# Another order for the whole kernel, and the second block's selected row gathered by a register index

## The chip, the cores and the metric

The kernel runs on one core of one Trainium2 chip. The metric is the device time of one execution in microseconds (us), as the median of the runs. Before the change three runs took 164.52, 165.06 and 165.21 us; the median is 165.06.

## The reference, cut to what matters

`x` has 2048 tokens (S) of 512 numbers (D), in bf16. Two kinds of block alternate, A, B, A, B, each on a layer norm of `x` with the result added to `x`. The weights are the same in both rounds.

```python
def _A_ref(x, wqkv, wo):                # linear attention, H = 32 heads of Dh = 16
    q, k, v = ...                       # x @ wqkv, split into heads
    phi = lambda t: jnp.where(t > 0, t + 1, jnp.exp(t)) + 1e-6
    pq, pk = phi(q), phi(k)
    kv = jnp.einsum("bhsd,bhse->bhde", pk, v)
    z = jnp.einsum("bhsd->bhd", pk)
    num = jnp.einsum("bhqd,bhde->bhqe", pq, kv)
    den = jnp.einsum("bhqd,bhd->bhq", pq, z)[..., None] + 1e-6
    return (num / den) ... @ wo

def _B_ref(x, w_r, w_gate, w_up, w_down):   # one token of 2048 goes through an FFN
    r = x @ w_r
    idx = jnp.argsort(-r, axis=-1)[:, :1]
    x_sel = ...                         # row idx of x
    y = (silu(x_sel @ w_gate) * (x_sel @ w_up)) @ w_down      # F = 1792
    y = y * sigmoid(r[idx])
    return x + (y added to row idx)

x = x + _A_ref(_layernorm(x), ...);  x = x + _B_ref(_layernorm(x), ...)
x = x + _A_ref(_layernorm(x), ...);  x = x + _B_ref(_layernorm(x), ...)
```

## The kernel before, in words

**Layout.** The 2048 tokens are 16 tiles of 128 (`x_tok[:, t, :]`, tokens on partitions). `xn_tok` holds the normalised tiles, `xnT[0]` and `xnT[1]` the transposed ones for block 0 and block 1, `pqT` the transposed phi(q), `pk` a ring of six phi(k) tiles. In PSUM six banks (0 to 5) go round for everything short, and two (6 and 7) are held by accumulations.

**How the order is made.** Each piece of work is an operation of the recorder `Sched` (`add`), with the tiles that it reads and writes. `replay` puts all 1047 operations in the order of a list of numbers, `ORDER`, and gives each PSUM buffer the bank that the string `BANKS` names. `assign_sync` then makes one stream per engine and the semaphore waits between streams, and `emit_engine` writes the streams out. So each engine, and the DMA queue of SyncE (SP), runs its operations strictly in the order of `ORDER`; whoever waits holds up everything behind it on that engine. The names below are those that the code gives operations, with the tile or group number: `A0k13` is block 0's key product of tile 13.

**Start and block 0, keys (`ln0`, `T_pe`, `T_dma`, `kv_tile`).** SP loads `x` in four pieces, the three 512x512 parts of `wqkv` (wk, wv, wq), `wo` and the router weight. For each tile VectorE (DVE) takes the statistics (L825, L827), ScalarE (ACT) the scale; the normalised tile comes from DVE for tiles 0 to 3 (L814) and from GpSimd (POOL, L818) for the other twelve, for pairs of tiles at a time. Tiles 0 to 3 are transposed by TensorE (PE, L804), the other twelve by a DMA transpose on SP (L435, `A0T4` to `A0T15`), which can be issued once POOL has made the tile. The key product (L618, four 128x512 matmuls) needs the transposed tile; then phi: ACT's exp (L552, `E`), POOL's min (L554, `min`), DVE's max and add (L556, `phi`). In block 0 no value product is made: `gmm` (L641, L645) adds the Gram product of the normalised tile with phi(k) into four banks, with a column of ones for z. These banks are complete after all 16 tiles.

**Block 0, queries to output.** Query products in groups of four tiles (L781, `A0q{group}_{chunk}`, phi as above); the denominator of a group (`den`, L906), whose reciprocal goes through DRAM to all partitions (`rd_scr`, `rb_sb`) and is multiplied into `pqT` (L925, `qd`). `kv_out` makes the kv product from the Gram banks (`GT`, then L715 with wv), masks it (`kvTe`, L719), and `m_out` folds `wo` in (L758, `Mw`). Output tiles (`out_tile`, L950; the router's columns ride along, L544), the residual (L975, `res`) and the sum of squares (L981). `ln_mid` makes the layer norm before the second half, with POOL's tiles and DMA transposes again (`A1T`).

**FFN weights.** w_gate, w_up and w_down come in six pieces of 0.92 MB (`ldwg0`, `ldwg1`, `ldwu0`, ...), on SP too. They may be issued once `A0T15` has landed (the argument `after=[hold]`).

**Block B of the first round** (`b_front(0, ...)`, `coupling`) runs beside block 1's key and value products: the largest router value over 16 tiles (DVE MAX8 and FIND_INDEX8), over partitions by a PE transpose of the maxima, the same again; a one-hot column; POOL loads the tile index into a register and copies the selected tile to `xg` (L1133), and PE gathers the row from it (L1141, `B0gather`); `tots` (L1174), `xm`, `xsel`; the gate and up rows on PE (L1222, `B0row_g`, `B0row_u`); the down row; then the change of one token is patched into block 1 as a rank-2 update of the kv sums (`Crank2`) and added to `x` by POOL (`Cxpatch`).

**The tail: block B of the second round** (`cand_front`, `b_front(1, ...)`, `final_row`). When the last two output tiles are done, the router row is complete and the FFN of the selected token is all that is left. The row of the token is gathered in two parts. `cand_front` searches the first `NA = 12` tiles alone, ahead of time: MAX8 (L1071), the transpose of the maxima (L1073), FIND_INDEX8 (L1075, L1079), a one-hot table (`oha`, L1080), and 48 one-column matmuls over all 12 tiles (L1090). `b_front(1, ...)` searches all 16 (L1099 to L1108) and gathers from the last four tiles by 16 one-column matmuls (L1146). A fourth statistic, a flag of the first 12 tiles, tells whether the candidate is the token; `gx` joins the parts. Then `xsel`, 112 one-column matmuls for gate and up (L1204), 112 for the down row (L1283), the row's copy (L1435) and its store at a row index that SP loads into a register (L1440, L1445). That store waits for all eight output stores.

Of the kernel before, what the change touches and what calls it, by code (L numbers as in the profile page):

```python
# [6 lines left out]
dt = mybir.dt  # L7
# [4 lines left out]
P = 128  # L12
# [13 lines left out]
3 24 0 11 19 25 54 18 1 30 20 7 21 12 56 31 33 27 2 61 9 55 10 8 53 76 6 57 78 58 77 79 62 80 81 63 82 64 85  # L26
65 83 66 60 84 99 67 86 101 68 59 100 102 69 154 103 104 87 105 70 88 106 164 71 72 155 73 107 23 90 165 74
156 169 75 89 91 108 157 92 4 159 93 110 170 166 109 94 158 167 160 97 134 29 168 171 98 132 161 172 184 95
123 173 96 133 135 162 136 137 189 185 112 111 186 138 145 163 190 141 187 179 113 22 121 142 139 114 115 188
124 116 180 143 191 140 146 117 192 174 144 181 39 147 193 175 118 122 119 182 148 125 227 149 176 40 126 196  # L30
120 152 177 183 228 41 127 153 222 229 47 262 223 230 150 5 178 48 263 151 202 264 306 224 265 231 203 128 225
207 204 129 246 205 208 226 209 130 210 232 197 247 131 206 38 49 233 310 237 234 32 311 248 211 235 307 238
308 28 249 239 217 309 240 236 218 195 50 258 242 219 15 259 220 241 260 243 26 261 244 212 245 254 213 200
221 214 194 255 215 256 250 13 257 266 251 199 216 252 34 51 267 253 268 270 315 312 269 331 271 316 274 332
272 52 286 275 273 333 198 390 287 334 290 276 201 391 35 282 392 277 288 291 393 294 14 289 313 292 283 278
46 314 295 284 293 298 279 296 285 335 317 280 299 297 281 300 302 318 394 435 303 301 325 323 436 326 304 319
437 321 305 320 438 327 322 483 324 42 338 484 328 329 336 346 485 339 330 337 486 340 396 347 349 43 397 348
341 343 439 350 342 402 398 351 344 370 408 395 345 403 487 399 372 409 373 374 405 371 375 400 404 441 352
376 442 401 447 354 377 440 410 443 444 406 378 355 379 356 380 411 489 357 453 383 445 358 407 488 450 384
359 381 454 360 361 446 353 413 492 362 479 44 365 451 414 382 455 448 495 363 452 366 490 415 569 491 416 417  # L40
493 501 364 523 418 480 412 419 496 420 570 498 421 502 449 422 494 562 368 426 499 423 456 497 458 555 571 45
427 572 548 556 386 544 528 563 559 557 389 549 428 558 459 552 460 457 550 429 461 560 573 564 551 462 500
424 545 594 553 431 385 463 481 425 387 504 464 465 554 574 466 580 565 469 527 503 506 367 566 467 475 36 507
470 369 508 37 509 505 477 473 524 581 576 510 529 468 430 471 530 587 577 511 525 519 521 567 16 472 578 601
434 588 579 531 512 561 513 590 532 514 602 520 660 517 533 597 534 546 661 535 518 667 664 536 595 583 537
668 662 665 540 591 670 568 598 618 592 541 584 515 593 671 615 619 672 585 474 611 538 586 673 575 516 620
675 622 616 543 674 599 676 612 582 432 680 677 539 604 542 600 613 678 621 589 605 681 653 683 682 623 686
679 606 687 625 691 688 614 684 608 607 626 689 627 596 609 690 632 743 696 717 646 633 722 654 685 603 634
694 692 610 628 647 643 476 697 695 635 648 699 655 703 720 700 719 701 639 704 693 644 705 702 617 649 707
706 708 657 698 709 640 710 711 656 624 641 658 712 666 716 642 650 713 714 744 526 659 651 715 636 723 724  # L50
725 522 726 637 629 727 728 732 729 17 652 730 638 731 547 645 741 735 748 736 630 737 752 738 749 739 776 750
753 751 760 754 777 478 756 778 779 631 757 740 755 772 761 758 813 814 762 768 759 773 718 812 763 764 769
774 829 770 765 775 788 830 771 766 784 831 721 767 789 832 815 867 785 669 790 780 868 786 791 792 869 787
781 870 816 482 793 742 782 804 745 794 783 817 796 746 795 805 833 824 797 905 825 820 906 798 821 800 806
907 799 822 801 818 908 807 808 819 871 826 802 823 827 733 663 828 809 835 834 841 810 803 837 838 811 836
943 842 909 847 944 388 839 945 844 849 873 946 875 843 879 872 845 848 885 874 846 880 840 851 855 911 876
850 881 852 912 734 853 910 882 854 886 947 859 913 877 920 887 858 883 878 914 860 921 884 861 917 888 747
922 915 864 890 923 916 893 863 918 891 949 866 892 919 433 856 955 889 948 924 931 951 897 950 925 952 898
896 927 894 902 926 956 895 900 928 958 929 971 957 932 857 972 953 862 930 962 933 966 899 959 954 865 991
901 934 960 967 935 992 993 968 963 969 904 970 982 964 995 903 980 983 994 973 997 981 965 975 984 996 986  # L60
1001 998 961 1002 1003 936 999 976 1005 939 1004 1007 1006 987 1008 937 1011 1016 940 1017 974 938 1015 942
977 1018 1012 1000 985 941 1022 1009 988 1023 1024 1014 1033 1025 1013 989 1019 1040 990 1041 1020 1026 978
1021 979 1027 1028 1029 1035 1030 1042 1036 1031 1034 1037 1032 1038 1043 1039 1044 1045 1010 1046
"""
BANKS = "2403150522641073114052325233233533225255235115320324135406723415020315045210301352254130541121053023253414550523104221121142345331250413420510350421143216203317204426531407436254125010354"
# [186 lines left out]
def bass_interleave_layers__linear_attn_block__moe_arch_mod__prompt_kernel(  # L252
# [13 lines left out]
    with ExitStack() as es:  # L266
# [9 lines left out]
        NA = 12  # L276
# [102 lines left out]
        m8a = SB("m8a", [P, 8], BF)  # L379
        i8a = SB("i8a", [P, 8], dt.uint32)  # L380
        g8a = SB("g8a", [P, 8], F32)
        gi8a = SB("gi8a", [P, 8], dt.uint32)
        tifa = SB("tifa", [P, 1], F32)
        ohta = SB("ohta", [P, NA], F32)
        oha = SB("oha", [P, NA], BF)
        gca = SB("gca", [P, NC_D], F32)
        gx = SB("gx", [P, NC_D], F32)
# [32 lines left out]
        reg_sp = es.enter_context(nc.sync.register("reg_sp"))  # L420

# [71 lines left out]
        C("pool", lambda e: e.memset(stat[1][:, 3, :], 0.0), ["flag"], est=100)  # L493
        C("pool", lambda e: e.memset(stat[1][:, 3, 0:NA], 1.0), ["flag"], est=100)
# [571 lines left out]

        def cand_front():

            sl = slice(0, NA)
            res = [f"r{g[0]}" for g in FG if g[0] < NA]  # L1070
            small(lambda e: e.max(m8a[:], r_bf[:, sl]), res, ["m8a"], "B1Amax", est=170)  # L1071
            rowb = bank()
# [8 lines left out]
                                                   scalar=iota_p[:, 0:1], in1=ohta[:], op0=ALU.is_equal,  # L1081
                                                   op1=ALU.mult), ["gi8a", "ohta", "iota_p"], ["oha"], "B1Aoh",
                  est=230)
            ga = bank()

            def gather_a(e):
                ins = None
# [483 lines left out]
```

## Time and profile before

| what | us |
|---|---|
| median of three runs | 165.06 |
| the profiled execution | 164.52 |
| its span, first to last instruction | 162.7 |
| PE busy | 148.8 |
| DVE busy | 132.9 |
| ACT busy | 106.2 |
| POOL busy | 75.2 |
| first key product of block 0 | 9.15 |
| first output tile of block 0 | 58.8 |
| first output tile of block 1 | 131.4 |
| last dense product | 149.2 |
| gate products of the tail | 154.80 |

The profile is of one execution. Its page gives the busy time of each engine, the span in 40 slices of 4.07 us (a digit is the busy share in tenths; below them the clock that TensorE was granted and the DMA engines' share), the chain of work that ended last, and groups of equal instructions with what ended the idle time before them. Other views are asked of the trace for a window of time: the timeline (start, length, engine, line, operation, output <- inputs, count), the list of waits (who waited for whom: total, times, longest), the DMA issues with their time to landing, and a table by stage. A line such as `L618` is a line of the kernel before. A helper's line stands for many operations: L571 is every small three-operand instruction of DVE. PE is the stream of matmuls, PEld that of weight loads beside it; a 512-column matmul shows as 0.38 us long, but the next one starts 0.22 us after it.

### The profile page before, as it was taken

How to read it: one execution, taken by the hardware profiler on the slowest of the kernel's cores; microseconds unless marked ns; L12 is line 12 of the kernel's file. 1: busy time of each engine (PE TensorE's matmuls, PEld its weight loads, DVE VectorE, ACT ScalarE, POOL GpSimd, SP SyncE). 2: the span in 40 equal slices, each digit the busy share in tenths (PEclk: the TensorE clock that was granted, in tenths of full speed). 3: DMA queues.
4: the chain of work that ended last, by engine and by line, in shares of the span. 5: the costliest groups of instructions: out<-in, count | busy, mean ns of one | idle time of the engine just before them, and what ended most of it. 6: DMA issues, size and time to landing. Idle time of an engine off the chain costs nothing.

```text
span 162.7 us, 3493 instructions
## 1 busy us (share of the span) xinstructions
PE 148.8 (91%) x1281; PEld 71.4 (44%) x1163; DVE 132.9 (82%) x452; ACT 106.2 (65%) x282; POOL 75.2 (46%) x125
## 2 busy tenths in 40 slices
PE   7989999999999969999999989799999979997593
PEld 2434444444434434334344535465444323332582
DVE  2999998677999999998784696784586999999951
ACT  3493453344489667977989537445779929997950
POOL 2058788744357500255875936630496710154000
PEclk9999999999999999999999999999999999999855
DMA  4999543769986767333334430000004687421360
GB/s 142 328 378 249 119 101 61 244 146 376 366 303 212 245 231 224 129 71 79 78 69 74 91 62 0 4 4 2 0 0 147 236 266 240 137 78 64 146 242 7
DMA packets 31633, 24.21 MB, mean 149 GB/s; under 512 B 15872, under 2 KB 30080, under 8 KB 31488
## 3 DMA queue, kind: packets, MB, share of 16 engines
q1 hardware_dynamic: 31616, 23.99, 49.2%
q8 instruction: 9, 0.15, 0.4%
q14 instruction: 8, 0.07, 0.2%
HBM read 14.03 MB, written 6.29 MB: 125 GB/s over the span
## 4 chain that ended last, share of the span: by engine, by line
DVE 36%; PE 32%; DMA 14%; ACT 9%; POOL 3%; issue 3%; SPq 1%; DVEq 0%
PE ps L618 11%; PE ps L781 6%; DVE x_tok L975 6%; DVE pqT L556 5%; DVE pqT L925 5%; DMA rb_sb<-rd_scr 5%; DMA x_tok<-in_A_x_dram 3%; PE ps L660 3%; PE ps L641 3%; DMA xnT<-xn_tok 3%; DMA rd_scr<-rden 3%; DVE pk L556 3%; DVE junk L851 3%; ACT Eb L552 2%; PE ps L1204 2%
## 5 line engine op out<-in xcount | busy, mean ns | idle before, releaser
L554 POOL TENSOR_SCALAR Eb<-Eb 128x512 bf16<-128x512 bf16 x64 | 40.3, 638 | 29.3 <-ACT Eb L552 28.6
L552 ACT ACTIVATE Eb<-ps 128x512 bf16<-128x512 f32 x64 | 37.1, 596 | 24.2 <-PE ps L618 15.0
L618 PE MATMUL ps<-wqkv,xnT 128*128 128x512 bf16 x153 | 38.3, 379 | 2.2 <-DVE pk L556 0.6
L950 PE MATMUL ps<-Mw,pqT 128*128 128x512 bf16 x124 | 31.1, 378 | 2.3 <-DVE pqT L925 1.4
L781 PE MATMUL ps<-xnT,wqkv 128*128 128x512 bf16 x123 | 29.6, 380 | 0.4 <-ACT Eb L552 0.2
L556 DVE SCALAR_TENSOR_TENSOR pk<-ps,Eb 128x512 bf16<-128x512 f32 x32 | 21.7, 681 | 6.7 <-POOL Eb L554 6.6
L556 DVE SCALAR_TENSOR_TENSOR pqT<-ps,Eb 128x512 bf16<-128x512 f32 x32 | 21.1, 683 | 5.6 <-POOL Eb L554 5.6
L950 PEld LDWEIGHTS ps<-Mw,pqT 128*128 128x128 bf16 x128 | 12.2, 96 | 20.9 <-DVE pqT L925 3.2
L818 POOL TENSOR_SCALAR xn_tok<-x_tok,stat,nms 128x512 bf16<-128x512 bf16 x16 | 12.4, 784 | 17.9 <-DVE nms L1017 14.7
L618 PEld LDWEIGHTS ps<-wqkv,xnT 128*128 128x128 bf16 x160 | 13.5, 97 | 15.5 <-DVE pk L556 1.3
L781 PEld LDWEIGHTS ps<-xnT,wqkv 128*128 128x128 bf16 x128 | 11.5, 97 | 13.9 <-issue 1.1
L981 ACT ACTIVATE junk<-x_tok 128x512 bf16<-128x512 bf16 x26 | 16.1, 620 | 2.2 <-DVE x_tok L975 1.8
L641 PE MATMUL ps<-pk,xn_tok 128*128 128x512 bf16 x64 | 16.4, 379 | 0.1
L544 PE MATMUL ps<-mr_hl,pqT 128*128 128x2 bf16 x96 | 15.8, 164 | 0.2
L925 DVE TENSOR_TENSOR pqT<-pqT,rb_sb 128x512 bf16<-128x512 bf16 x32 | 13.7, 447 | 0.7 <-DMA rb_sb<-rd_scr 0.7
L818 POOL TENSOR_SCALAR xn_tok<-x_tok,rs,nms 128x512 bf16<-128x512 bf16 x12 | 10.2, 850 | 8.5 <-DVE mv L827 8.0
L825 DVE BATCH_NORM_STATS2 st<-x_tok 128x6 f32<-128x512 bf16 x16 | 10.6, 677 | 2.2 <-DMA x_tok<-in_A_x_dram 2.1
L680 ACT ACTIVATE va<-ps 128x512 bf16<-128x512 f32 x16 | 9.5, 592 | 4.2 <-PE ps L618 2.7
L975 DVE SCALAR_TENSOR_TENSOR x_tok<-x_tok,ps 128x512 bf16<-128x512 bf16 x16 | 10.7, 677 | 0.0
L791 ACT ACTIVATE lnv<-mv,eps_col 128x2 f32<-128x2 f32 (+2 forms) x20 | 5.8, 291 | 7.2 <-DVE mv L827 6.4
L1426 POOL TENSOR_SCALAR xn_tok<-x_tok,us,stat 128x512 bf16<-128x512 bf16 x6 | 4.8, 803 | 11.9 <-DVE stat L571 9.9
L641 PEld LDWEIGHTS ps<-pk,xn_tok 128*128 128x128 bf16 x64 | 6.2, 97 | 7.3
(256 smaller groups left out, 232.8 us busy)
## 6 DMA issues: line engine op xcount, KB each, us to landing
rd_scr<-rden SPq DMA_DIRECT2D x8, 512.0 KB, 3.7
rb_sb<-rd_scr SPq DMA_DIRECT2D x8, 512.0 KB, 3.9
out_dram<-xn_tok SPq DMA_DIRECT2D x8, 256.0 KB, 2.1
wg<-in_B_w_gate_dram SPq DMA_DIRECT2D x2, 896.0 KB, 13.9
wu<-in_B_w_up_dram SPq DMA_DIRECT2D x2, 896.0 KB, 7.8
wd<-in_B_w_down_dram SPq DMA_DIRECT2D x2, 896.0 KB, 9.8
wqkv<-in_A_wqkv_dram SPq DMA_DIRECT2D x3, 512.0 KB, 6.0
x_tok<-in_A_x_dram SPq DMA_DIRECT2D x1, 1024.0 KB, 8.9
```

The lines of the kernel that those rows point to most:

```text
L544: ins = e.matmul(out_ap, lhsT, rhs, start=start, stop=stop, skip_group_check=True).ins
L552: A("act", lambda e: e.activation(Eb[:, i, :], src(), ACTF.Exp), reads=[b, "table"], writes=[f"E{i}"], est=600, name=name + "E")
L554: A("pool", lambda e: e.tensor_scalar(Eb[:, i, :], Eb[:, i, :], 1.0, 0.0, op0=ALU.min, op1=ALU.max), reads=[f"E{i}"], writes=[f"E{i}"], es ...
L556: return A("dve", lambda e: e.scalar_tensor_tensor(out=dst, in0=src(), scalar=1e-6, in1=Eb[:, i, :], op0=ALU.max, op1=ALU.add), reads=[b, ...
L618: ins = e.matmul(B(b), xT[:, c, t * P:(t + 1) * P], wqkv[:, c, lo:lo + D], start=(c == 0), stop=(c == NC_D - 1))
L641: e.matmul(B(kba[c]), xn_tok[:, t, c * P:(c + 1) * P], pk[:, i, :], start=first, stop=False, skip_group_check=True)
L781: ins = e.matmul(B(qb), wqkv[:, c, qc * P:(qc + 1) * P], xnT[L][:, c, tg * 512:(tg + 1) * 512], start=(c == 0), stop=(c == NC_D - 1))
L818: A("pool", lambda e: e.tensor_scalar(xn_tok[:, t, :], x_tok[:, t, :], scale[:, t:t + 1], nbias[:, t:t + 1], op0=ALU.mult, op1=ALU.add), r ...
L925: A("dve", (lambda e, tc=tc, rc=rc: e.tensor_tensor(pqT[:, :, tc], pqT[:, :, tc], rb_sb[:, i, :, rc], ALU.mult)), reads=[f"rb{i}"] + [f"pq ...
L950: ins = e.matmul(B(ob), w, Mw[:, m, :], start=(m == 0), stop=(m == NC_D - 1 and not xb))
L975: A("dve", lambda e: e.scalar_tensor_tensor(out=x_tok[:, t, :], in0=x_tok[:, t, :], scalar=scal, in1=B(ob), op0=ALU.mult, op1=ALU.add, acc ...
L981: A("act", lambda e: e.activation(junk[:, j, :], x_tok[:, t, :], ACTF.Square, accum_out=s2[L][:, t:t + 1]), reads=[f"x{t}", "table"], writ ...
```

## The change

1. **The second round's gather.** `cand_front` goes away, with its tiles, its flag (two POOL fills) and the join `gx`. `b_front(1, ...)` loads the tile index into a register of PE and gathers the row with four one-column matmuls whose weights are the selected tile, addressed by that register. The number of statistics falls from four to three.
2. **A new `ORDER` and a new `BANKS`** for all that is left, 1034 operations. Nothing else in the code differs; the lines after the removed ones move up by 11 (L618 becomes L607, and so on).

The core of the diff (the two long strings left out):

```diff
-        NA = 12
...
+        reg_pe = es.enter_context(nc.tensor.register("reg_pe"))
...
-        C("pool", lambda e: e.memset(stat[1][:, 3, :], 0.0), ["flag"], est=100)
-        C("pool", lambda e: e.memset(stat[1][:, 3, 0:NA], 1.0), ["flag"], est=100)
...
-        def cand_front():
-            ...
-            small(lambda e: e.max(m8a[:], r_bf[:, sl]), res, ["m8a"], "B1Amax", est=170)
...
-                for c in range(NC_D):
-                    for t in range(NA, NT):
-                        ins = e.matmul(B(gb)[:, c:c + 1], x_tok[:, t, c * P:(c + 1) * P], oh_bf[:, t:t + 1],
-                                       start=(t == NA), stop=(t == NT - 1))
+            def gather_reg(e):
+                e.reg_load(reg_pe, idxu[0:1, 1:2])
+                gregs["t"] = index(e, reg_pe, NT)
...
                 for c in range(NC_D):
+                    src = xg[:, c * P:(c + 1) * P] if L == 0 else x_tok[
+                        :, bass.ds(gregs["t"], 1), c * P:(c + 1) * P].rearrange("p a d -> p (a d)")
+                    ins = e.matmul(B(gb)[:, c:c + 1], src, ohp_bf[:, 0:1], start=True, stop=True)
...
+                A("pe", gather, reads=["idxu1", "ohp_bf"] + [f"x{t}" for t in range(NT)], writes=[gb], est=1050,
+                  pre=gather_reg, pre_after=[idx1_op], name=tag + "gather")
-            nr = 4
+            nr = 4 if L == 0 else 3
...
-                stt(gx[:], gca[:], tots[:, 3:4], ALU.mult, lambda: B(gb)[:, 0:NC_D], ALU.add, ["gca", "tots", gb],
-                    ["gx"], tag + "gx")
-                stt(xsel[:], gx[:], tots[:, 0:1], ALU.mult, tots[:, 1:2].to_broadcast([P, NC_D]),
-                    ALU.add, ["gx", "tots"], ["xsel"], tag + "xsel")
+                stt(xsel[:], lambda: B(gb)[:, 0:NC_D], tots[:, 0:1], ALU.mult, tots[:, 1:2].to_broadcast([P, NC_D]),
+                    ALU.add, [gb, "tots"], ["xsel"], tag + "xsel")
```

What the two orders make of the streams, by the names of the operations (`ld` are loads, `T` the DMA transposes of block 0):

```
SP before: ldx2 ldx0 ldx4 ldwk ldx8 ldwo ldwq ldwrb T6 ldwv T7 T5 T4 T13 T12 T8 T9 T15 ldwr T14
           ldwg0 T10 T11 ldwu1 ldwd1 ldwu0 ldwd0 ldwg1
SP after:  ldx0 ldx2 ldx4 ldwk ldx8 ldwq T7 T6 ldwrb T8 T5 T4 T9 T11 T15 T10 ldwo T14 T12
           ldwd1 ldwu1 ldwg0 T13 ldwd0 ldwg1 ldwu0 ldwr ldwv

PE before: pT2 pT0 pT3 k0 k2 pT1 k3 k1 kv0 kv2 k6 kv3 k7 kv1 k5 kv6 k4 kv7 k13 kv5 k12 q1_1 kv4 k8
           kv13 k9 q0_1 kv12 k14 kv8 k15 kv9 k11 kv14 q1_0 q0_0 kv15 k10 q0_3 kv11 q0_2 q1_2 kv10
           q1_3 den0 q2_0 q2_3 den1 q3_0 q2_2 q3_1 q2_1 q3_2 kvT q3_3 den2 M3 M2 M0 M1 den3
PE after:  pT0 pT2 k0 pT3 pT1 k2 k1 k3 kv0 kv2 k7 kv1 kv3 k6 k8 kv7 k5 kv6 k4 k9 kv8 kv5 k11 q0_0
           k15 kv9 kv4 k10 kv15 k14 k12 q0_1 kv11 k13 kv14 kv12 q0_2 q0_3 kv10 kv13 q1_3 q1_2 q1_0
           q1_1 den0 q2_3 q2_1 den1 q2_0 q3_0 q2_2 q3_1 q3_3 q3_2 kvT den2 M1 M2 M0 M3 den3

POOL after, during block 0's key products: ... k4min k9min xn14 xn12 k11min q0_0min k15min xn13 ...

PE, first selection, before: kv8 v13 row_g row_u k13 tr_g kv9 tr_u v15 kv10 row_y
PE, first selection, after:  gather kv8 tot v14 kv6 row_g row_u v11 tr_g k14 tr_u k12 row_y
DVE, there, before: tots Cinv u3 xm k11phi (statistic) x2c xsel k12phi
DVE, there, after:  tots xm xsel rl_g k13phi rl_u k11phi u3 x2c

PE, into block 1's outputs, before: rank2 q1_2 q1_1 q1_0 den0 ... M0 q3_3 Ctw wo1 wo0 den3 wo3
PE, into block 1's outputs, after:  rank2 kv12 q1_0 q1_1 den0 ... M0 Ctw den3 wo2 wo1 wo3
PE, tail, after:  rowmax tsel tot (register load) gather g0 u0 g7 u7 row_x row_y
DVE, tail, after: ... max mi tif gmax oht gmi (statistic) oh oht_p psf prod ohp idx1 (tile) ... tots ...
                  xsel (tile) (tile) ...
```

In these streams `pT` is a PE transpose, `k`, `v`, `q` key, value and query products, `kv` in block 0 the Gram product of a tile, `wo` an output tile.

## The prediction

> **What bounds the kernel now.** I read the page first: busy shares, the 40 slices, the chain that ended last. No engine is the bound throughout; TensorE (PE) and VectorE (DVE) take turns, and PE is rarely idle for long before the tail.
>
> ```profile
> PE 148.8 (91%) x1281; PEld 71.4 (44%) x1163; DVE 132.9 (82%) x452; ACT 106.2 (65%) x282; POOL 75.2 (46%) x125
> PE   7989999999999969999999989799999979997593
> DVE  2999998677999999998784696784586999999951
> ```
>
> PE is at 9 in nearly every slice up to the tail; DVE is loose in slices 6 to 9 (24 to 41 us) and full after. So an idle PE before 41 us is paid in full if DVE has nothing to give back, and the body's order matters more than a few small instructions.
>
> Next I read the DMA queue, because the change reorders it. First the view of DMA issues in the window 18 to 29 us, then in 29 to 32 us (name, count, us to landing), then SP's timeline.
>
> ```profile
> xnT<-xn_tok SPq DMA_TRANSPOSE x6, 2.5
> ```
> ```profile
> xnT<-xn_tok SPq DMA_TRANSPOSE x1, 4.1
> ```
> ```profile
> 26.91 1.21 SPq L435 DMA_TRANSPOSE xnT<-xn_tok  x1
> 28.17 0.58 SPq L437 DMA_DIRECT2D wg<-in_B_w_gate_dram  x1
> 29.55 4.07 SPq L435 DMA_TRANSPOSE xnT<-xn_tok  x2
> ```
>
> A block-0 transpose lands 2.5 us after its issue when nothing is ahead of it. The one issued at 29.55, behind one 0.92 MB gate load, took 4.1 and landed at 33.65. The table by stage (window, length, PE PEld DVE ACT POOL busy, clock, DMA share, GB/s) shows why: the load ramps up over two us, fills the engines, and only then does the transpose move.
>
> ```profile
> 29.00:30.00 1.00, 0.92 (x9) 0.53 (x9) 0.51 (x1) 0.12 (x1) 1.00 (x2) 1.00 0.55 56
> 31.00:32.00 1.00, 1.00 (x10) 0.51 (x9) 0.32 (x1) 0.00 (x0) 0.97 (x2) 1.00 1.05 405
> 32.00:33.00 1.00, 1.00 (x10) 0.47 (x8) 1.00 (x4) 0.59 (x1) 0.40 (x1) 1.00 1.07 309
> 38.00:39.00 1.00, 1.00 (x7) 0.41 (x5) 1.00 (x4) 0.47 (x1) 0.00 (x0) 1.00 1.08 382
> ```
>
> **Part 1, the new place of one transpose: +2.5 us.** In the changed order SP issues twelve block-0 transposes as before, but the last, of token tile 13, stands behind *three* weight loads (half of w_down, of w_up, of w_gate). Key product k13 is PE's 16th key product and needs it; PE runs in order.
>
> When does it land? One load ahead: issue of the load at 28.17 to landing of the transpose at 33.65 is 5.5 us. Each further 0.92 MB at the 373 GB/s of 36 to 44 us (same table) adds 2.5. Three ahead: 5.5 + 2 x 2.5 = 10.5 us after the first load's issue. That issue follows the transpose of tile 12, whose normalised tile POOL makes after the min of k9. In the new PE order nine key products and six Gram products precede k9; counting from 9.15 (the first key product) with PE's rows below and two input transposes of 0.33, k9 starts at 9.15 + 9 x 0.86 + 6 x 0.96 + 0.66 = 23.3 and ends at 24.2. Then exp 0.6, min 0.61, two POOL tiles at 0.78 each: 27.0; the transpose keeps SP 1.2: 28.2. With 0.4 for hops and contention the first load issues at about 28.6 and tile 13 lands at 39.1 (38.2 if the ramp hides behind the wo load, 40 if SP or POOL slip).
>
> When does PE want it? PE's timeline, the pattern of the first 40 us:
>
> ```profile
> 31.02 1.03 PE L641 MATMUL ps<-pk,xn_tok 128*128 128x512 bf16 x4
> 31.88 0.24 PE L645 MATMUL ps<-ones_bf,pk 128*128 128x1 bf16 x4
> 31.98 1.02 PE L618 MATMUL ps<-wqkv,xnT 128*128 128x512 bf16 x4
> 40.16 1.02 PE L618 MATMUL ps<-wqkv,xnT 128*128 128x512 bf16 x4
> ```
>
> A Gram product with its ones column costs 0.96 from start to start, a key or query product 0.86. The last key product of before starts at 40.16, after 15 keys, 14 Grams, 4 queries; k13 of the changed order comes after 15, 12, 2. So PE is ready at 40.16 - 2 x 0.96 - 2 x 0.86 = 36.5. It waits 39.1 - 36.5 = 2.6; I take 2.5, bounds 1.7 and 3.7. What PE saves at the front (two waits for transposes at 15 and 17 us, 0.5 together, since the wo and wv loads leave their way) is swallowed by this wait. It is not given back: from 40.16 to 54.4 PE of before shows no wait over 0.4 us, and the block's kv product, mixed matrix and output tiles all need k13's Gram. DVE does its constants during the wait, but PE is the bound there.
>
> A second price could be PE's clock. The table by stage for PE alone (window, length, busy, clock, DMA, GB/s) shows one fall, in the tail, some 4.5 us after the last dense product:
>
> ```profile
> 152.00:153.00 1.00, 1.00 (x44) 1.00 0.38 135
> 153.00:154.00 1.00, 0.79 (x22) 0.83 0.00 0
> 154.00:155.00 1.00, 0.38 (x14) 0.50 0.55 207
> ```
>
> A wait of 2.5 is shorter than that, so I add nothing. The Trainium skill (TensorE: Matmul & The Clock Gate, Part 1) says that one idle window of about 3.4 us halves PE's clock. By it a wait of 2.5 would cost nothing more, and one of 3.7 could add up to 1.7, as an estimate.
>
> The same skill (DMA: Bandwidth & Descriptors, Anatomy of one DMA) fits a transfer as 2.0 us plus bytes / 436e3. As an estimate three loads would take 2.0 + 3 x 2.1 = 8.3, tile 13 would land near 38 and the wait be 1.4; the rows of this trace say more, and they decide.
>
> **Part 2, other moves in the body: -0.8 us.** Two waits of before that the new order touches, from the lists of waits in 100 to 104 and 118 to 132 us:
>
> ```profile
> PE ps L1222 <- DVE xsel L571: 0.7, 1, 0.7
> ```
> ```profile
> PE ps L950 <- DVE pqT L925: 0.9, 1, 0.9
> ```
>
> The first: before the gate rows DVE does key product k11's phi, x2c and a statistic between xm and xsel. In the new order xsel follows xm, and PE has a value product and a kv product (0.86 + 0.23) beside them: -0.7. The second: block 1's first denominator waited 0.4 for phi; now one product fewer stands between the rank-2 patch and it, so its DRAM round trip starts earlier: -0.4 to -1.3. Against: the y row has one kv product less beside its gate (+0.3), kvT of block 0 has no query product after it (+0.1), and any new order brings waits of its own. Sum of the named ones about -1.1; taken -0.8, bounds -2.2 and +1.0.
>
> **Part 3, the selection of block 1: +0.15 us.** Removed: nine DVE operations of the candidate search and of the join, 48 + 16 one-column gathers, two POOL fills. The 48 (1.35 us) lie inside DVE's chain, where PE is idle: 0. Of the DVE ones, MAX8 and FIND_INDEX8 (0.07 + 0.15 of the chain) stand ahead of tile 15's statistics and one at 0.14 ahead of the global MAX8; the rest run while ACT makes the row scale or PE the row: -0.3 (0 to -0.5).
>
> Added: the gather now needs the tile index in a PE register. From the end of the last FIND_INDEX8 (152.59) to the gate products (154.80) takes 2.21 now. New path: oh 0.2, oht_p 0.22, PE 0.25, idx1 0.15 with two hops of 0.05 (0.9 in all, as psf, prod and ohp stand ahead of idx1 but end first), register load, four register operations with weight loads, matmul and hop 0.25, xsel 0.25. A register load on PE is not in the trace. The nearest rows, of idxu:
>
> ```profile
> L1131 POOLq TENSOR_LOAD <-idxu x1: 487/487/487, 96.8 to 96.8; - x1
> L1304 POOLq TENSOR_LOAD <-idxu x1: 303/303/303, 98.4 to 98.4; - x1
> L1440 SPq TENSOR_LOAD <-idxu x1: 575/575/575, 156.5 to 156.5; - x1
> ```
>
> I take 0.49, the load that a compute engine does first; 0.3 and 0.58 are the ends. A matmul addressed by register is not there either: a register operation takes 0.04 to 0.06 on POOL, so 4 x (0.05 + 0.1) = 0.6, at most 1.0. Sum 0.9 + 0.49 + 0.6 + 0.25 + 0.25 = 2.5, against 2.21: +0.3 (0 to +0.8). Behind the waiting load on PE stand only the FFN products, which need xsel anyway; prod's total is ahead of it. With -0.3 and a little for the smalls that follow the phis in the new order: +0.15, bounds -0.5 and +0.8. The FFN itself (112 one-column products and 112 rows back to back, 154.80 to 160.0) is the same work. The row's store waits for the output stores too: the last landed at 160.4, the row was ready at 160.34. DVE's last tiles move up, so the stores don't become the end.
>
> **Sum.** 2.5 - 0.8 + 0.15 = +1.9. The profiled execution took 164.52 (span 162.7, 1.8 around it), giving 166.4; it is the fastest of the three, 0.54 under the median. On the median of 165.06: **167.0 us**.
>
> **Rivals.**
> - *Tile 13 comes in time.* For: the three loads have no consumer before the gate rows at 102.8 us, and if a transpose passes what is queued ahead, part 1 is 0. It decides if the first load issues before 36.5 - 10.5 = 26.0, or packets of the two mix. Against: the 4.1 us row, and POOL's place of tile 12. Then the sum is -0.65: 164.4; with all of part 2's gain 163.0. Chance 0.2, half of it faster than now.
> - *The wait is longer and the clock falls.* At 3.7 the wait comes near the 4.5 us after which the tail's clock fell; each 512-column product (0.22) would take twice as long for some 3 us: +1.5 over the long end: 165.06 + 3.7 + 1.5 - 0.65 = 169.6, 168.8 with half of it. Chance 0.1. Against: PE is never idle for 2 us in the body, so no row shows it.
> - *The wait is there and is given back.* Part 1 at its low end, part 2 at its high end: 165.06 + 1.7 - 2.2 + 0.15 = 164.7, to 165.8. Chance 0.1.
> - The forecast: 0.6, own range 165.9 to 168.6.
>
> **Chances.** About 0.5% (0.8 us) is what a measurement of this kernel can tell from no change. Faster 0.10, same 0.20, slower 0.70. The range 164.2 to 168.9 leaves out the fast half of the first rival and the long end of the second.
>
> **What would show it.** Part 1: the transposes' longest time to landing is 8 us or so, and PE stands idle 2 to 3 us before one key product at 36 to 39 us, ended by a DMA of xnT. Right in kind but wrong in size if the idle is under 1.5. Wrong if no PE idle over 1 us lies before 45 us. Part 2: no wait of the gate rows for xsel. Part 3: from the last FIND_INDEX8 to the gate products 2.3 to 3.0 us.

## The result, and the profile after

The changed kernel takes 171.44 us (median of four runs, 170.37 to 171.77), the kernel before 165.07 beside it: 1.038 times as long, 95% interval 1.033 to 1.043. The prediction said 167.0, at most 168.9: right in sign, a third of the size. The profiled execution took 171.77 us, its span is 170.0 against 162.7. Ratios here and below leave out executions over 1.5% above the fastest of their kernel; medians count all of them.

From the page of the changed kernel, the lines that answer to those of before:

```profile
PE 147.9 (87%) x1220; PEld 70.4 (41%) x1102; DVE 126.1 (74%) x441; ACT 105.3 (62%) x282; POOL 75.4 (44%) x123
PE   7999499990699995989999999999999979998293
DVE  2999689577047699979983399475685998899951
PEclk9999999999599999999999999999999999999755
```

All engines but POOL have slightly less work. PE has two holes, a 4 in the fifth slice (17 to 21 us) and a 0 in the tenth (38 to 42.5 us). In the eleventh the granted clock falls (the 5), which in the kernel before it did only in the tail; its line was

```profile
PEclk9999999999999999999999999999999999999855
```

The second hole first. SP's timeline (start, length, operation, output <- input), then the DMA issues of that window (name, count, us to landing), then PE's timeline:

```profile
32.03 0.58 SPq L428 DMA_DIRECT2D wd<-in_B_w_down_dram  x1
32.65 0.56 SPq L428 DMA_DIRECT2D wu<-in_B_w_up_dram  x1
33.26 0.51 SPq L428 DMA_DIRECT2D wg<-in_B_w_gate_dram  x1
33.81 2.93 SPq L426 DMA_TRANSPOSE xnT<-xn_tok  x1
```
```profile
xnT<-xn_tok SPq DMA_TRANSPOSE x1, 9.8
```
```profile
43.77 1.86 PE L607 MATMUL ps<-wqkv,xnT 128*128 128x512 bf16 x4 [5.53 <-DMA xnT<-xn_tok]
```

The last line is key product k13, as predicted: behind three loads the transpose of tile 13 takes 9.8 us, and PE stands. But it stands 5.53 us, not 2.5. PE by stage (window, length, busy, clock, DMA, GB/s) shows what comes after:

```profile
42.00:43.00 1.00, 0.00 (x0) 1.00 0.63 75
44.00:45.00 1.00, 1.00 (x3) 0.50 1.09 348
46.00:47.00 1.00, 1.00 (x6) 0.64 1.06 383
```

The clock is halved from 43.31 to 46.72 by the record of the granted clock. The products there take nearly twice their time: k13, above, 1.86 us for 1.03.

The first hole is before k8, which needs tile 8. The list of waits, 14 to 30 us (total, times, longest):

```profile
PE ps L607 <- DMA xnT<-xn_tok: 2.2, 1, 2.2
```

The prediction had no wait there. Tile 8's transpose is issued at 15.58 and lands at 20.39: 4.8 us, though no weight load is near; only `ldwrb`, the broadcast of the router row, stands ahead of it. What held it is in the DMA issues of 17.5 to 19.5 us: the engines' busy tenths in 40 parts of the window, then a queue named "instruction" (packets, MB, share).

```profile
DMA  4649949999000009990000000001011000000000
q8 instruction: 1, 0.02, 3.0%
```

One 16 KB packet of program code, at 17.87 us for 0.96, shares the DMA engines with the transposes. In the first line the engines are busy to 18.0 us and once more for a moment at 18.25, then there is next to nothing until the end of the window. The packets of the trace, one by one, say more: none starts between 18.35 and 18.82, and from the end of the code packet (17.87 + 0.96 = 18.83) the rest start one after the other, some 0.03 us apart, up to 19.6. So the tile is held until the code packet is done. Which of the 16 engines carried what the trace does not give; that the code packet held up one of them is argued. In the kernel before such a packet comes at 18.43 and falls in a gap between two transposes (same view, 17.5 to 20 us):

```profile
DMA  9941000000000090000000000000000000000004
q8 instruction: 1, 0.02, 2.9%
```

**Where the 7.3 us of the span went**, from the starts of the same products in both traces: first output tile of block 0 at 67.69 for 58.79, 8.9 later; from there to the last output tile of block 1 87.2 for 88.8, 1.6 shorter; from there to the end 15.11 for 15.13, the same. All of the loss is made before 47 us.

### The profile page after: what moved, and what is told of

Read it like the earlier page. It is cut to its first block, busy times and chain, and to the rows that moved or that the text cites. A ratio compares the mean times of both kernels' runs of the same rounds, so it can differ in the third digit from the quotient of the medians.

```text
span 170.0 us, 3350 instructions
## 1 busy us (share of the span) xinstructions
PE 147.9 (87%) x1220; PEld 70.4 (41%) x1102; DVE 126.1 (74%) x441; ACT 105.3 (62%) x282; POOL 75.4 (44%) x123
## 4 chain that ended last, share of the span: by engine, by line
PE 40%; DVE 25%; DMA 16%; ACT 14%; issue 2%; POOL 1%; SPq 0%; DVEq 0%
PE ps L607 13%; PE ps L770 8%; DMA xnT<-xn_tok 7%; PE ps L630 6%; DMA rb_sb<-rd_scr 6%; DVE x_tok L964 6%; DVE pqT L914 5%; ACT Eb L541 4%; PE ps L526 4%; ACT junk L970 3%; DMA rd_scr<-rden 2%; DVE pqT L545 2%; ACT va L669 2%; PE ps L1161 2%; DVE pk L545 2%
## 5 line engine op out<-in xcount | busy, mean ns | idle before, releaser
L543 POOL TENSOR_SCALAR Eb<-Eb 128x512 bf16<-128x512 bf16 x64 | 39.6, 626 | 46.1 <-ACT Eb L541 45.9
L541 ACT ACTIVATE Eb<-ps 128x512 bf16<-128x512 f32 x64 | 37.6, 596 | 33.8 <-PE ps L607 23.2
L607 PE MATMUL ps<-wqkv,xnT 128*128 128x512 bf16 x155 | 39.4, 385 | 8.8 <-DMA xnT<-xn_tok 7.7
L545 DVE SCALAR_TENSOR_TENSOR pk<-ps,Eb 128x512 bf16<-128x512 f32 x32 | 21.4, 681 | 10.7 <-POOL Eb L543 10.5
L545 DVE SCALAR_TENSOR_TENSOR pqT<-ps,Eb 128x512 bf16<-128x512 f32 x32 | 21.6, 687 | 9.6 <-POOL Eb L543 9.3
L607 PEld LDWEIGHTS ps<-wqkv,xnT 128*128 128x128 bf16 x160 | 13.6, 98 | 23.8 <-issue 6.3
L807 POOL TENSOR_SCALAR xn_tok<-x_tok,stat,nms 128x512 bf16<-128x512 bf16 x16 | 13.0, 814 | 17.8 <-DVE mv L984 12.3
L914 DVE TENSOR_TENSOR pqT<-pqT,rb_sb 128x512 bf16<-128x512 bf16 x32 | 13.2, 440 | 1.6 <-DMA rb_sb<-rd_scr 1.6
L1383 POOL TENSOR_SCALAR xn_tok<-x_tok,us,stat 128x512 bf16<-128x512 bf16 x6 | 5.6, 938 | 11.4 <-DVE tot L560 9.2
L964 DVE SCALAR_TENSOR_TENSOR x_tok<-x_tok,ps 128x512 bf16<-128x512 bf16 x16 | 10.5, 677 | 0.0
## 6 DMA issues: line engine op xcount, KB each, us to landing
wg<-in_B_w_gate_dram SPq DMA_DIRECT2D x2, 896.0 KB, 11.3
```

What stands on the lines that cost most here:

```text
L541: A("act", lambda e: e.activation(Eb[:, i, :], src(), ACTF.Exp), reads=[b, "table"], writes=[f"E{i}"], est=600, name=name + "E")
L543: A("pool", lambda e: e.tensor_scalar(Eb[:, i, :], Eb[:, i, :], 1.0, 0.0, op0=ALU.min, op1=ALU.max), reads=[f"E{i}"], writes=[f"E{i}"], es ...
L545: return A("dve", lambda e: e.scalar_tensor_tensor(out=dst, in0=src(), scalar=1e-6, in1=Eb[:, i, :], op0=ALU.max, op1=ALU.add), reads=[b, ...
L607: ins = e.matmul(B(b), xT[:, c, t * P:(t + 1) * P], wqkv[:, c, lo:lo + D], start=(c == 0), stop=(c == NC_D - 1))
L807: A("pool", lambda e: e.tensor_scalar(xn_tok[:, t, :], x_tok[:, t, :], scale[:, t:t + 1], nbias[:, t:t + 1], op0=ALU.mult, op1=ALU.add), r ...
L914: A("dve", (lambda e, tc=tc, rc=rc: e.tensor_tensor(pqT[:, :, tc], pqT[:, :, tc], rb_sb[:, i, :, rc], ALU.mult)), reads=[f"rb{i}"] + [f"pq ...
```

## The experiments

Edits of the order are shown as the stream of SP or PE by name. Each kernel is measured beside runs of the kernel before on the same chip (medians 163.48, 164.83, 164.19 and 164.46 for the four groups, in the order below).

### First group: the waits one by one

```diff
 t13_first
-SP: T12 ldwd1 ldwu1 ldwg0 T13 ldwd0
+SP: T12 T13 ldwd1 ldwu1 ldwg0 ldwd0
```

> The changed kernel with one edit: the transpose of tile 13 is issued ahead of the three weight loads, not behind them. Theory (its landing at 43.6 us is a wait of 5.5 us of PE, and the halved clock after it costs 1.7 more): both go, about 171.4 - 7.2 = 164.2 us; the transpose lands some 2.5 us after its issue, PE has no idle over 1 us before that key product, the granted clock stays at 1.0. Rival (PE would have waited there or later for something else, because the new order of block 0 is slow by itself): 168 to 171 us.

Measured: 166.99, ratio 1.0144 (1.0045 to 1.0242). The wait for tile 13 is gone, but 1.4% is left. Its list of waits, and the clock in slices of 4.1 us:

```profile
PE ps L607 <- DMA xnT<-xn_tok: 2.1, 1, 2.1
PEclk9999969999999999999999999999999999999755
```

The wait that is left is the one before k8, and in this execution it cost a fall of the clock (21.55 to 24.97) which the same wait did not cost in the changed kernel. Two things more follow later: the loads end 2.4 us later, and output tiles of block 0 wait 1.4 for denominators.

```diff
 t13_warm (k13 stays behind the loads)
+        gram = next(o for o in sch.ops if o.name == "A0kv11").banks[0]
+        def warm13(e):
+            for _ in range(22):
+                e.matmul(B(gram), zeros[:, 0:P], zeros[:, :], start=False, stop=False, skip_group_check=True)
+        k13.pre = warm13
```

> The changed kernel with 22 matmuls of zeros (512 columns each, 4.8 us, added into the Gram banks, so they change no value) on PE while it waits for tile 13; the wait itself stays. Theory (the idle PE loses its clock, and that costs 1.7 us apart from the wait): no fall of the clock at 43 us, about 169.8 us. Rival (the slow clock costs nothing, since DVE and ACT set the pace after the wait): 171.2 to 171.6 us. Rival (matmuls beside the loads slow the transpose): over 172.

Measured: 168.93, 1.0312 (1.0222 to 1.0403). The clock stays at full speed up to the tail in the trace, and from k13 to the first output tile the kernel needs 1.4 us less (22.5 for 23.9). The halved clock is a cost of its own, in the trace somewhat under the 1.7 expected; the times say 1.1 us (1.0381 to 1.0312), with intervals that overlap.

```diff
 wrb_late; "both" is this and t13_first
-SP: T6 ldwrb T8 T5 T4 T9 T11
+SP: T6 T8 T5 T4 T9 ldwrb T11
-DVE: k7phi wsum ... k6phi r0d10 ... k5phi r0d14
+DVE: k7phi ... k6phi ... k5phi wsum r0d10 r0d14
```

> The changed kernel with the broadcast load of the router weight issued behind the transpose of tile 9, not ahead of that of tile 8, and DVE's first two readers of it moved behind phi of tile 5. Theory (this load holds the transpose of tile 8 up by 2.3 us, PE stands before k8, and all that follows up to the three loads comes later by as much): tile 8 lands 2.5 us after its issue, PE's wait before k8 goes from 2.2 to under 0.3, the first weight load is issued 2.3 us earlier, the wait for tile 13 stays 5.5: about 169.1 us. Rival (the wait for tile 13 absorbs it, since the loads' time is bound by transfers): 171.4.

> Both edits: tile 13 ahead of the three loads, router weight behind tile 9. Theory: 171.4 - 7.2 - 2.3 = 161.9 us, 3 us below the kernel before; what is left of the new order is then a gain of 0.9 in front, 1.6 in the body and nothing in the tail. Rival (the two waits overlap, and each repair alone already brings all that is to be had): 164.2.

Measured: 173.10, 1.0562 (1.0484 to 1.0639), and 166.62, 1.0156 (1.0071 to 1.0241). Both theories of mine fell here. With `ldwrb` out of its way k8 still came at 19.87 instead of 20.44, so the broadcast load is not the main cause of that wait. The late sums on DVE made a new wait: query product q0_0 stood 1.0 for `wmean`. In the first of the two the loads then went out at 33.05 and the clock was halved for two windows (42.55 to 49.38).

### Second group: the packet of code, the denominators, the tail

```diff
 t13_fetch: t13_first, and in warm(n)
-                for _ in range(n):
-                    ins = e.matmul(B(b), zeros[:, 0:P], zeros[:, :], start=True, stop=True)
+                for c in range(4 * n):
+                    lo = (c % 4) * P
+                    ins = e.matmul(ps[:, b.idx, lo:lo + P], zeros[:, 0:P], zeros[:, lo:lo + P], start=True, stop=True)
 t13_den: t13_first, and
-SP: T13 ldwd1 ldwu1 ldwg0 ldwd0 ldwg1 ldwu0 ldwr ldwv rw0 ... rb3
+SP: T13 ldwr ldwv ldwd1 ldwu1 ldwg0 ldwd0 rw0 ... rb3 ldwg1 ldwu0
```

(`rw`, `rb` are the writes and reads of the denominators; t13_den_fetch has both edits.)

> Tile 13 ahead of the three loads, and each 512-column warm-up matmul of zeros at the start cut into four of 128 columns: 108 PE instructions more before the first product, so that the 16 KB packet of instructions that the trace shows at 17.8 us, among the packets of tile 8's transpose, comes some 8 us earlier. Theory (that packet keeps one of the DMA engines for 1 us and then leaves 64 packets of two transposes behind on it, so tile 8 lands at 20.3; PE's wait of 2.1 us before k8 halves the clock for 3.4 us from 21.5): tile 8 lands at about 18.9, the wait falls to 0.8, the clock stays: 1.5 + 1.3 = 2.8 us less than the first repair, ratio 0.997. Rival (the broadcast load of the router weight alone makes tile 8 late): as the first repair, 1.014.

> Tile 13 ahead of the three loads, and two more edits on SP's queue: the router row and wv are issued right behind tile 13, and the last two weight loads (w_gate, w_up) behind the four denominator round trips of block 0. Theory (with tile 13 repaired, the loads end 2.4 us later than in the changed kernel, the first denominator write then takes 5.7 us to land instead of 3.3, and two output tiles wait for the denominators by 1.0 and 0.7): the writes land in 3.3 us again, these waits go, about 1.0 us under the first repair, which was 1.014 times the kernel before: 1.008. Rival (the round trips are late for another reason): 1.014.

> All of it: tile 13 ahead of the loads, wv and router row early, two loads late, the packet of instructions moved. Theory: 2.8 + 1.0 under the first repair, ratio 0.991 to the kernel before, so the new order without its three collisions on the queues is somewhat faster than the old. Rival (the new order has no gain of its own in the body): 1.00 or more.

Measured: t13_fetch 163.14, **0.9903 (0.9864 to 0.9941)**; t13_den 165.69, 1.0072 (1.0035 to 1.0109); t13_den_fetch 163.85, 0.9985 (0.9934 to 1.0035).

In t13_fetch the packet comes at 11.54. Its DMA issues in 11 to 13 us hold it, and those of 16 to 17 us show tile 8's transpose:

```profile
q8 instruction: 1, 0.02, 3.5%
```
```profile
xnT<-xn_tok SPq DMA_TRANSPOSE x1, 2.7
```

2.7 us to landing for 4.8, with `ldwrb` still ahead of it; PE has no wait over 0.2 us left in the list of 14 to 45 us. The other traces of the changed order agree. Where `ldwrb` stands ahead of tile 8 and the first packet comes at 17.6 to 18.1 (after, t13_first, t13_warm, t13_den), the tile lands after 4.7 to 4.8 us; where it comes at 11.0 to 12.8 (the seven kernels with the cut warm-up), after 2.7 to 3.3. So the packet was the cause, and moving it was worth 2.4% on top of the first repair (1.0144 to 0.9903). By the traces the span is 3.2 shorter (165.2 to 162.0): 1.4 us are the start of k8 (20.31 to 18.89), 1.5 lie between the starts of k8 and k13 (17.58 us for 19.05), where the clock of t13_first was halved, and the denominators are no longer late. The first output tile comes 3.1 earlier (62.02 to 58.95).

Two things in the trace of t13_fetch are easy to overlook. The cut moves the second packet too: it starts at 30.2 to 31.4 us in the seven kernels, for 42.8 to 48 without the cut, and there it meets the transposes of tiles 14 and 12. They land after 5.3 to 5.7 and 3.7 to 4.6 us, for 3.9 to 4.4 and 2.4 to 2.9 in the traces without the cut. PE waits at most 0.3 for that. And the clock did fall once in the body, later:

```profile
PEclk9999999999999978999999999999999999999655
```

It was halved from 58.84 to 62.26. In the window before that (55.43 to 58.84) PE had been busy for 1.82 of 3.41 us, without a wait over 1.03.

In t13_den the denominators' writes come through; DMA issues of 46 to 66 us, t13_first and then t13_den:

```profile
rd_scr<-rden SPq DMA_DIRECT2D x4, 512.0 KB, 5.3
```
```profile
rd_scr<-rden SPq DMA_DIRECT2D x4, 512.0 KB, 3.3
```

That held, and the ratio is as expected, though its interval overlaps that of t13_first. The sum of both did not hold: with the packet moved the loads end 4 us earlier anyway (wv lands at 52.2 for 56.3), so there was nothing left to repair, and the two late loads now lie ahead of block 1's first transposes (4.3 us to landing; PE waits 0.9).

```diff
 tail_only: the kernel before up to A1wo15, then the changed tail
-PE: ... A1wo15 Arow rowmax Agather tot gather(16 columns) tsel g7 g0 u0 ...
+PE: ... A1wo15 rowmax tsel tot (register load) gather(4 columns) g0 u0 g7 u7 ...
```

> The kernel before with the order of before up to its last output tile, and from there the changed tail: candidate search left out, gather by a register index, the changed kernel's order. Theory (the tail is worth nothing: the traces show 15.1 us from the last output tile to the end in both): ratio 0.997 to 1.003. Rival (the register load and the four register operations on PE cost more than the candidates save): 1.003 to 1.006.

Measured: 164.08, 0.9937 (0.9894 to 0.9979). The tail costs nothing; the rival falls, and the ratio lies under the range expected too. In the trace the end comes at 162.7 as before, so the gain of the times is unexplained, and I do not count on it. It matters all the same: 0.9937 is as much as the whole new order gains without its waits (0.9903 here, 0.9933 when repeated below), so by the times the gain of the body's order is not separated from that of the tail.

### Third group: alone, a control, the cause in the old order

fetch_alone is the changed kernel with the cut warm-up and tile 13 left where it is; before_fetch the kernel before with the same cut.

> The changed kernel with the warm-up matmuls cut as before and nothing else; tile 13 stays behind its three loads. Theory (two separate waits in a row: tile 8, made by the packet of instructions, and tile 13, made by the queue): k8 starts 1.4 us earlier, so do POOL's tiles and the three loads, tile 13 lands 1.4 earlier, PE's wait for it stays 5.5 and the clock falls there as before: 1.4 us off, ratio 1.030. Rival (the wait for tile 13 swallows what comes earlier): 1.038.

> The kernel before with its warm-up matmuls cut in the same way: a control. Theory (in the old order the packet of instructions at 18.4 us falls on transposes that nothing waits for): 0.997 to 1.003. Rival (the cut warm-up is a gain by itself, through the clock or the start, whatever the order): 0.99, as in the changed order with its first repair.

Measured: fetch_alone 170.76, 1.0407 (1.0332 to 1.0481); before_fetch 164.40, 1.0027 (0.9987 to 1.0067). So the cut warm-up is no gain by itself. It is not without an effect: the first packet now comes at 12.29, among the old order's transposes, and one key product waits for it (14 to 18 us):

```profile
PE ps L619 <- DMA xnT<-xn_tok: 1.1, 1, 1.1
```

The first output tile comes 1.0 later, counted from the first key product, and the times don't show it. fetch_alone is a miss. Its trace does what was expected (k8 at 18.91, first load at 30.14, k13 at 41.72 for 43.77) and the profiled execution is 2.4 us shorter, but the four executions (169.41 to 172.16, granted clock 0.959 down to 0.938) gain nothing. Its list of waits (the cut adds a line to the code, so L608 is L607 of the changed kernel):

```profile
PE ps L608 <- DMA xnT<-xn_tok: 5.4, 3, 4.9
```

```diff
 before_t11 (on the kernel before)
-SP: ldwg0 T10 T11 ldwu1 ldwd1 ldwu0
+SP: ldwg0 T10 ldwu1 ldwd1 T11 ldwu0
```

> The kernel before with one edit: the weight loads ldwu1 and ldwd1 are issued ahead of the transpose of tile 11 and not behind it, so that it stands behind three loads. Theory (a transpose waits 2.5 us for each load ahead of it, PE stops for it, and nothing is given back): tile 11 lands 10.5 us after the first load's issue, at 38.7, PE stands 3.2 us before k11: ratio 1.019, or 1.03 if the clock falls too. Rival (the old order has slack at this place and takes the wait up): under 1.01.

Measured: 169.78, 1.0238 (1.0148 to 1.0329). The old order, with nothing but this, loses 2.4% (four executions, 167.45 to 171.10). Waits (14 to 45 us) and clock of the profiled one, which is the longest of the four:

```profile
PE ps L618 <- DMA xnT<-xn_tok: 4.0, 2, 3.8
PEclk9999999995699999999999999999999999999655
```

Tile 11 landed at 39.1 (38.7 expected), 11.3 after the first load's issue, PE stood 3.8 before k11, and in this execution the clock was halved for two windows.

```diff
 best: t13_den_fetch, with the two late loads moved on
-SP: rb3 ldwg1 ldwu0 A1T1 ... A1T11 A1T13
+SP: rb3 A1T1 ... A1T11 ldwg1 ldwu0 A1T13
```

> Tile 13 ahead of the loads, wv and the router row right behind it, the warm-up cut, and the last two weight loads (w_gate, w_up) behind block 1's transpose of tile 11, where SP has nothing to issue for 4 us. Theory (with these two loads ahead of block 1's first transposes, those took 4.3 us and PE waited 0.9): that wait goes too, ratio 0.985 to 0.99. Rival (the loads now hold up the transposes of tiles 13 to 15 and the gate rows that need w_gate): 0.995 or more.

Measured: 164.00, 0.9975 (0.9936 to 1.0014). It is not the best: in its trace the gate rows of the first selection come 9.9 us after the row of maxima, for 8.6 in t13_den_fetch. The rival is right in its first half: a transpose issued behind the two loads, at 93.27, took 4.8 us, and PE waited 1.2. Its second half, gate rows that wait for their weights, did not happen: w_gate had landed at 95.2, and the gate rows came at 102.4.

### Fourth group: what was still open

fetch_warm is fetch_alone with the 22 matmuls of zeros of t13_warm; t13_fetch2 is t13_fetch again.

```diff
 t13_two (warm-up cut)
-SP: T12 ldwd1 ldwu1 ldwg0 T13 ldwd0
+SP: T12 ldwd1 ldwu1 T13 ldwg0 ldwd0
```

> The changed kernel with both of its clock and packet repairs and not the third: the warm-up cut, so that the packet of instructions comes early, and 22 matmuls of zeros on PE while it waits for tile 13; tile 13 stays behind its three loads. Theory (the packet costs 1.5 us, the fall of the clock 1.7 to 2.4, the wait for tile 13 stays): ratio 1.031, which the matmuls of zeros alone gave, less 1.5 us: 1.022. Rival (the cut warm-up gives nothing while tile 13 is late, as the time of that edit alone said): 1.031.

> The changed kernel with the warm-up cut and tile 13 behind two weight loads, not three (w_gate goes behind it). Theory (2.5 us for each load ahead, and PE free at 36.5): tile 13 lands at 39.0, PE waits 2.5 us, where three loads gave 4.9 and none gave no wait; ratio 0.990 + 0.015 = 1.005 where no window of the clock is lost, 1.015 where one is. Rival (the wait depends on the load that is under way alone, not on how many stand in the queue): 1.03 as with three.

> The kernel with tile 13 ahead of the loads and the cut warm-up once more, unchanged, in five rounds. Theory (its two causes of loss are gone and the rest of the new order is worth 1 to 1.6 us): 0.988 to 0.995. Rival (its 0.990 was a lucky set of executions): 0.997 or more.

Measured: fetch_warm 169.25, 1.0240 (1.0164 to 1.0316); t13_two 167.30, 1.0085 (1.0039 to 1.0131); t13_fetch2 163.17, **0.9933 (0.9901 to 0.9965)**.

With the clock kept, moving the packet gives the expected ratio, but the interval overlaps that of t13_warm, and the traces do not decide it either. Beside the changed kernel, fetch_alone is 1.5 earlier at k8 and 2.2 earlier at the first output tile; beside t13_warm, fetch_warm is 1.8 earlier at k8 and only 0.2 earlier at k13 (43.35 for 43.54) and at the first output tile. In fetch_warm tile 13 landed 13.2 us after the first load's issue, for 11.2 in t13_warm; the DMA issues of 31.5 to 34.5 us show its transpose:

```profile
xnT<-xn_tok SPq DMA_TRANSPOSE x1, 10.3
```

So whether the two waits add while tile 13 stays behind the loads is open. Where tile 13 is repaired, moving the packet is worth 2.4% by the times as well: the intervals of t13_first and t13_fetch don't overlap. t13_fetch2 repeats t13_fetch: the new order without its two waits is 0.3 to 1.0% faster than the kernel before. In t13_two tile 13 lands 8.8 us after the first load's issue, where three loads gave 11.4 and one, in the kernel before, 5.5: about 3.0 us for each load. Its wait:

```profile
PE ps L608 <- DMA xnT<-xn_tok: 2.4, 1, 2.4
```

This is the wait of the prediction, 2.4 us. Its twelve executions run from 164.39 to 169.65 (their median is 1.7% above that of the kernel before), and the three fastest were granted 0.968 to 0.972 of the clock, the three slowest 0.946 to 0.953. The one traced execution kept the clock up to the tail. That a wait of this length halves the clock in some executions and not in others is likely by these numbers, and no trace of t13_two shows it; t13_fetch2, without the wait, ranges from 0.954 to 0.973.

## Why the prediction was wrong, point by point

**Part 1, +2.5: the mechanism right, the size wrong.** Its terms, beside the changed kernel and the one with the packet out of the way:

| term (us) | predicted | after | fetch_alone |
|---|---|---|---|
| first load issued | 28.6 | 32.03 | 30.14 |
| tile 13 lands after that | 10.5 | 11.6 | 11.4 |
| PE ready for k13 | 36.5 | 38.24 | 36.78 |
| wait | 2.6 | 5.5 | 4.9 |

The step that failed is "with 0.4 for hops and contention the first load issues at about 28.6". Of its error of 3.4, 1.9 is the wait before k8 (POOL's tiles follow k8, and with them tile 12 and the loads); PE is late by nearly as much, so this part mostly adds in series. The other 1.5 is in the chain behind k9: in fetch_alone k9 starts at 23.45 (23.3 worked out), but its min ends at 26.45 (25.4), and POOL's tile 12 takes 1.45 us, not 0.78. The price of a load was 2.5 by the table of before; it is 3.3 from one load to two and 2.7 from two to three, and the landing came 1.1 later than the 10.5 worked out. The upper bound of 3.7 was too tight: it was passed by 1.2 us in fetch_alone, where the chain of products, helpers and queue that it stood on slipped by 1.5 without any new wait. The estimate from the skill's fit is also mis-added: 28.6 + 8.3 is 36.9, not near 38, and the wait by it 0.4; and the page gives that fit for transfers that GpSimd issues, while these are issued by SP. Tile 13 landed 11.6 and 11.4 us after the first load's issue, so the rows of the trace were the better guide.

**"What PE saves at the front is swallowed."** It was not a saving: the front had a new wait of 2.2 before k8, which my working had not looked for. I had followed the loads that left the transposes' way and not those that came in (`ldwrb`), and had no view of the code packets at all, which the DMA issues of before show.

**The clock, +0.** The reason given, that 2.5 is shorter than the 4.5 us of the tail, failed twice: the wait was 5.5, and even 2.1 us were enough in the trace of t13_first. The row that I read held the warning: in the grid window before the tail's fall (150.25 to 153.67) PE was still busy for 1.84 of 3.42 us, and no wait in it was longer than 2.2, so the 4.5 us were not an idle stretch. The same table has the row just ahead of those shown:

```profile
149.00:152.00 3.00, 0.74 (x13) 1.00 0.47 173
```

PE is busy for 0.74 of these 3 us and all of the next one, and then the clock falls. The rival "the wait is longer and the clock falls" had the right mechanism, a chance of 0.1, and 169.6 as its time.

**Part 2, -0.8: right in sign, half the size.** From the first output tile of block 0 to the last of block 1 the changed order saves 1.6, and 2.2 in t13_fetch2 (86.6 for 88.8). The wait of the gate rows for xsel is gone, as predicted.

**Part 3, +0.15: right.** From the end of FIND_INDEX8 to the gate products 2.56 (2.5 predicted), the register load 492 ns (0.49 taken); from the last output tile to the end 15.11 for 15.13, inside the bounds.

```profile
L1098 PEldq TENSOR_LOAD <-idxu x1: 492/492/492, 160.7 to 160.7; - x1
```

**The sum.** In the prediction's terms the first output tile of block 0 should have come at 58.8 + 2.5 = 61.3; it came at 67.69. Of these 6.4 us, 1.7 are PE ready late, 2.9 the wait above its 2.6, 1.4 the halved clock and 0.3 the rest. Against t13_fetch2, the same order without its two waits, the changed kernel reaches k8 1.9 later (start of k0 taken out), k13 5.7 more, and the first output tile 1.45 more for the clock: 9.0 us in three terms, where the prediction had 2.5 in one. Without its waits the new kernel gains 2.5 in span (162.7 to 160.2) and 0.3 to 1.0% in time. In the traces that gain lies in the body, as the tail takes 15.0 to 15.2 us in all of them; by the times alone it could be the tail's (tail_only). What stays open: how much of the k8 wait `ldwrb` adds to the packet (its removal alone moved k8 by 0.6), why tail_only was measured 0.6% faster, and whether the two waits add in the changed kernel.

## What to carry to other kernels

A transpose in the same queue behind weight loads of 0.92 MB lands about 3.0 us later for each (2.5 us after its issue with none; 5.5, 8.8 and 11.4 after the first load's issue with one, two and three); before moving one there, work out its landing and its consumer's start, each with an error of a few us, and ask what the shortest order of the queue would be. Look in the trace for everything that shares the DMA engines, code included: it comes at a place in the instruction stream and not at a time, so any new order puts it beside other transfers. A wait of PE of 2 us can halve the clock for a window of 3.41 us; that cost 1.4 to 1.5 us more where it was measured (t13_warm beside the changed kernel, t13_fetch beside t13_first). It doesn't always happen.

## What the runs showed of the hardware

**Code packets.** Each traced execution has nine 16 KB packets on the queue named instruction (ten in before_fetch), of 0.9 to 1.9 us each. 108 more PE instructions ahead of the first product moved the first one from 17.8 to 11.5 us. The Trainium skill (Runtime: NRT & Kernel Launch, Instruction fetch mechanics) says that an engine's instruction memory is refilled in blocks of 16 KiB by a DMA queue of the sequencer, and that crossing a block is mostly hidden. The size agrees. Hidden it was for PE's own instructions (the idle times of PE for which no wait is found are at most 0.3 us), and not for the transpose on the same DMA engines, where the measurement decides: 4.7 to 4.8 us to landing for 2.7 to 2.9 in the same order (3.3 in best), 1.4 to 1.5 us at k8, and in t13_first a window of the clock.

**The clock goes by a grid.** The record of the granted clock changes at whole multiples of 3.413 us after its first rise: 37.55 us later (11 times) in the changed kernel, 17.07 (5 times) in t13_first, and in the body each fall lasts one or two of them. A fall follows a window in which PE was partly idle: busy for 0.0 of 3.41 us in the changed kernel, 0.75 in before_t11, 1.32 in t13_first, 1.82 in t13_fetch. But windows with 1.50 (t13_two), 1.55 (fetch_warm), 1.76 (the changed kernel, 36.48 to 39.90) and 1.81 (t13_den) kept it, so the busy time of a window alone does not sort them, and no threshold is shown. The same wait of 2.1 to 2.2 before k8 lay inside one window in t13_first and cost the clock, across two in the changed kernel (busy 2.23 and 2.31) and did not, and inside one in t13_den (the 1.81) and did not. So where a wait lies on the grid is likely part of the answer, and not all of it. The grid's start differed between traces by up to 3 us (3.9 to 6.9 us after the span's start). The Trainium skill (TensorE: Matmul & The Clock Gate, Part 1) says that the window is 3413 ns long and free-running; the runs agree. It speaks of an idle window; here one that was 39% busy (t13_first) and one that was 53% busy (t13_fetch) came before a fall.
